# Gated attention and token-MLP on one core: block 0 of X by two transposing DMAs of 256 columns, and the first weights on ACT's queue

## The chip, the cores and the metric

The kernel runs on one core of a Trainium2 chip. The metric is the device time of one execution in microseconds (us); the time before is the median of three timed runs. Next to it there is one profiled execution, whose span (first to last instruction) and whose trace are used for everything that is said of single instructions.

Engines are named as the profile names them: PE is TensorE's matmul and PEld its weight load, DVE is VectorE, ACT ScalarE, POOL GpSimd, SP SyncE. A small q behind a name (SPq, ACTq) marks an instruction of that engine's sequencer, here the issue of a DMA.

## The reference

The input x has 2048 rows (tokens) of 512 columns, in bf16. Two branches are computed from it and mixed by a gate for each row.

```python
def reference(A_x, A_wqkv, A_wo, B_x, B_w1, B_b1, B_w2, B_b2, gate_w):
    x = A_x
    g = _sigmoid((x * gate_w).sum(-1, keepdims=True))
    a = _A_ref(x, A_wqkv, A_wo)
    b = _B_ref(x, B_w1, B_b1, B_w2, B_b2)
    return g * a + (1 - g) * b
```

Branch A is local attention: `qkv = x @ wqkv` (512 x 1536), 32 heads of 16; each token attends to 8 tokens at distances 0, 2, ... 14 behind it; softmax; then `@ wo` (512 x 512). Branch B is a layer norm of x over its columns, then an MLP over the token axis: `u = gelu(h^T w1 + b1)` with w1 of 2048 x 1792, then `u w2 + b2` with w2 of 1792 x 2048, transposed back.

## The kernel before, in words

The kernel lists its operations in Python, each with an engine, an estimated duration, and what it reads and writes (`A = sch.add` for instructions, `sch.dma` for transfers). A list scheduler (`_Sched`) then fixes one static order for each engine from these estimates, from dependences, and from some orders that are written out by hand (`chain(...)`), and puts semaphore waits where data cross engines. For the loads at the start the scheduler's own estimate of a landing is overridden by a number written in the code (`op_.lands = t_`). These numbers shape the planned order; on the chip every instruction waits for the real semaphores.

X lies in SBUF twice: as `X` (tokens on partitions, 16 tiles of 128) for the layer norm, and transposed as `XT` (columns on partitions, 4 pieces of 128 columns, called d=0 to 3, by 2048 tokens) for the projections. XT comes straight from HBM by transposing DMAs, one for each block of 512 tokens: block 0 by `ld_xt0` (L467), blocks 1 to 3 by `ld_xt` (L460). Every other load goes through L429.

TensorE's program in order:

- warm-up matmuls on constants into a PSUM bank that nobody reads yet (L525): nine of 512 columns and one of 256;
- the first projections of block 0 (L593, operations `pf_...`): 8 accumulators, Q and K with 4 output parts each. The Q part goes column piece by column piece: 4 matmuls with d=0, then 4 with d=1, d=2 and d=3; then K with d=0 and 1 (8 matmuls) and with d=2 and 3 (8). So the first 4 matmuls want d=0 of Wq and of block 0, and so on;
- the projections of Q and K of block 1, then of blocks 2 and 3, then V (L593, `pj_...`), with two bursts that sum the attention products (L671);
- the MLP (L785, then L835), and the output projection Wo (L851).

ACT moves the projections out of PSUM (L601 for Q, L604 for K and V) and normalises X (L572). DVE takes the layer norm's statistics (L548, one for each tile of 128 tokens), multiplies Q by shifted K (L663), does the softmax and the weighted sum over V, and combines the branches (L872). DVE's order is written by hand: the statistics of X tiles 0 to 3 come first, then the first product of L663 (`qkm_0_0_0`), which wants Q and K of blocks 0 and 1 evicted by ACT.

The loads at the start, before the change, in the order of issue:

- ACT's queue: Wq, d=0 (`ld_w(0, 0, 1, "act")`);
- SP's queue: block 0 transposed (512 tokens x 512 columns), Wq d=1, d=2, d=3, Wk in two halves, X tiles 0 and 1, block 1 transposed, X tiles 2 and 3, X tiles 4 to 7, block 2, block 3, and the rest.

The two queues feed the same 16 DMA engines of the core. To keep SP's queue from running far ahead, each of SP's later loads waits for the landing of the one five places before it in a list (`throttle`, `init_dmas`).

Of the kernel before, what the change touches and what calls it, by code (L numbers as in the profile page):

```python
# [13 lines left out]
D = 512  # L14
# [4 lines left out]
NST = S // 128  # L19
# [314 lines left out]
def bass_gated_mix__sliding_local_dilated__mixer_token_mlp__prompt_kernel(nc, A_x, A_wqkv, A_wo, B_x, B_w1, B_b1, B_w2, B_b2, gate_w, out, dbg=None):  # L334
    with contextlib.ExitStack() as es:
        view, pview, off, total = _views(nc, es)
        ps = es.enter_context(nc.psum_tensor("ps", [128, 8, 512], FP32))
        esem = {e: es.enter_context(nc.semaphore("sem_" + e)) for e in ("pool", "act", "dve", "pe")}
        sch = _Sched()

        x2d = A_x[0]
# [7 lines left out]
        XT = view("XT", BF16, [(S, 4), (1, S)])  # L349
# [65 lines left out]
        A = sch.add  # L415
# [15 lines left out]
        init_dmas = []  # L431
# [4 lines left out]
        def prev_dma():  # L436
            return [init_dmas[-1]] if init_dmas else []

        def ld_x(t0, n, q="sp"):
            ds = sch.dsem("x%d" % t0)  # L440
            op = sch.dma(q, mk_dma(X[:, t0:t0 + n, :], xv[:, t0:t0 + n, :]), n * 128 * D * 2, ds,
                         writes=["x%d" % t for t in range(t0, t0 + n)], deps=throttle() if q == "sp" else [], after=prev_dma() if q == "sp" else [], name="d_x%d" % t0)
            if q == "sp":
                init_dmas.append(op)
            return op

        def ld_w(tn, d0, n, q="sp"):
            ds = sch.dsem("wqkv%d_%d" % (tn, d0))
            op = sch.dma(q, mk_dma(WQKV[:, d0:d0 + n, tn * D:(tn + 1) * D], wqkv_v[:, d0:d0 + n, tn * D:(tn + 1) * D]),
                         n * 128 * D * 2, ds, writes=["wqkv%d_%d" % (tn, dt) for dt in range(d0, d0 + n)],  # L450
                         deps=throttle() if q == "sp" and n == 4 else [], after=prev_dma() if q == "sp" else [],
                         issue=0.65 if n == 4 else 0.45, name="d_wp%d_%d" % (tn, d0))
            if q == "sp":
                init_dmas.append(op)
            return op
# [5 lines left out]
                         writes=["xt_%d" % t for t in range(4 * sb, 4 * sb + 4)], deps=throttle(), after=prev_dma(), name="d_xt%d" % sb)  # L461
            init_dmas.append(op)

        def ld_xt0(s0, s1):
            ds = sch.dsem("xt0_%d" % s0)
            dst = XT[:, :, s0:s1]
            op = sch.dma("sp", lambda e: e.dma_start_transpose(dst, x2d[s0:s1, :]), (s1 - s0) * D * 2, ds, issue=1.25,  # L467
                         writes=["xt_%d" % t for t in range(s0 // 128, s1 // 128)], after=prev_dma(), name="d_xt0_%d" % s0)
            init_dmas.append(op)
            return op  # L470

        first_loads = [ld_w(0, 0, 1, "act"), ld_xt0(0, 512), ld_w(0, 1, 1), ld_w(0, 2, 1), ld_w(0, 3, 1), ld_w(1, 0, 2), ld_w(1, 2, 2),
                       ld_x(0, 2)]
        ld_xt(1)
        first_loads.append(init_dmas[-1])
        for op_, t_ in zip(first_loads, (2.9, 4.9, 5.4, 5.8, 6.2, 7.0, 7.8, 8.6, 11.0)):
            op_.lands = t_
            op_.deps.clear()
        init_dmas[:] = [first_loads[1]] + first_loads[5:]
        ld_x(2, 2)  # L480
        ld_x(4, 4)
        ld_xt(2)
# [6 lines left out]
        def ld_w1(j):  # L489
# [4 lines left out]
            if j < 4:  # L494
# [8 lines left out]
                       writes=["wo"], deps=throttle(), after=prev_dma(), name="d_wo")  # L503
# [4 lines left out]
        for i_, (v_, n_) in enumerate(((B_b1, NFT), (B_b2, NST))):  # L508
            vr = v_.rearrange("(t q j) -> q t j", q=4, j=32)
            for q_ in range(4):  # L510
                sch.dma("sp", mk_dma(psub(BR, 32 * q_, n_, 32 * i_, [(1, 32)]), vr[q_]), n_ * 64, ds_b, reads=["br"],
                        writes=["br_%d_%d" % (i_, q_)], deps=throttle(), after=prev_dma(), name="d_b_%d_%d" % (i_, q_), issue=0.45)
        d_w1.append(ld_w1(3))
        A("dve", lambda e: e.transpose(out=BT, in_=BR), 0.2, reads=["br_%d_%d" % (i_, q_) for i_ in range(2) for q_ in range(4)],
          writes=["btc"], name="t_b")
# [2 lines left out]

        CONE = nc.const_aps.tensor(1.0, [128, D], BF16)

        def f_warm(n, w_=D):
            def fn(e):
                ins = None
                for _ in range(n):
                    ins = e.matmul(ps[:, 7, 0:w_], lhsT=CONE[:, 0:128], rhs=CONE[:, 0:w_], start=True, stop=True)  # L525
                return ins
            return fn

        A("pe", f_warm(9), 3.84, writes=["lg7_0", "lg7_1"], name="warm1", prio=-100)
        last_tx = A("pe", f_warm(1, 256), 0.2, writes=["lg7_0", "lg7_1"], name="warm2", prio=-100)  # L530

        ALLXT = ["xt_%d" % t for t in range(NST)]

        JK = view("OUTS", BF16, [(1, D)], extra=0)
        def cols(v_, lo, n, step=1):
# [9 lines left out]
        for hf in range(2):  # L545
            t0 = 8 * hf
            for t in range(t0, t0 + 8):
                A("dve", (lambda t_: (lambda e: e.bn_stats(out=ST6[:, t_, :], in_=X[:, t_, :])))(t), 0.59,  # L548
                  reads=["x%d" % t], writes=["st6_%d" % t], name="ln1_%d" % t, prio=0)
# [13 lines left out]
              reads=["zc%d" % hf], writes=["sd%d" % hf], name="ln_sqrt%d" % hf, prio=0)  # L563
            A("dve", (lambda t0_: (lambda e: e.reciprocal(out=cols(RSTD, t0_, 8), in_=cols(SD, t0_, 8))))(t0), 0.25,
              reads=["sd%d" % hf], writes=["rstd%d" % hf], name="ln_rstd%d" % hf, prio=0)
# [43 lines left out]
        for (b0, d0, d1, s0, s1) in ((0, 0, 1, 0, 512), (0, 1, 2, 0, 512), (0, 2, 3, 0, 512), (0, 3, 4, 0, 512), (4, 0, 2, 0, 512), (4, 2, 4, 0, 512)):  # L609
            for b in range(b0, b0 + 4):  # L610
                tn, dl = first[b]
                last_main[0] = A("pe", f_proj(tn, dl, 0, b, d0, d1, s0, s1), 0.216 * (d1 - d0) * (s1 - s0) / 512,
                                 reads=ALLXT[s0 // 128:s1 // 128] + ["wqkv%d_%d" % (tn, dt) for dt in range(d0, d1)],
                                 writes=fbn[b], after=[last_main[0]], name="pf_%s%d_%d_%d" % (tnames[tn], dl, d0, s0))
        for b, (tn, dl) in enumerate(first):
            A("act", f_evq(tn, dl, 0, b), 0.52, reads=fbn[b] + (["k5pad"] if tn == 1 else []),
              writes=["%s5_%d_0" % (tnames[tn], dl)], name="ev_%s%d_0" % (tnames[tn], dl), prio=0)
# [5 lines left out]
        for dl in range(4):  # L623
            seq_proj += [(2, dl, sb) for sb in range(4)]
        for (tn, dl, sb) in seq_proj:
            xr = ALLXT[4 * sb:4 * sb + 4]
            bank = main_bank()
            last_main[0] = A("pe", f_proj(tn, dl, sb, bank), 0.866,
                             reads=xr + ["wqkv%d_%d" % (tn, dt) for dt in range(4)],
                             writes=["acc%d" % bank], after=[last_main[0]], name="pj_%s%d_%d" % (tnames[tn], dl, sb), prio=0)  # L630
            A("act", f_evq(tn, dl, sb, bank), 0.62, reads=["acc%d" % bank] + (["k5pad"] if tn == 1 else ["v5pad"] if tn == 2 else []),
              writes=["%s5_%d_%d" % (tnames[tn], dl, sb)], name="ev_%s%d_%d" % (tnames[tn], dl, sb), prio=0)
# [11 lines left out]
                writes=["xa"] + ["wqkv%d_%d" % (tn, dt) for tn in range(3) for dt in range(4)], name="d_xa")  # L644
        for t in range(NST):
# [5 lines left out]
          writes=["th"], name="g_tanh", prio=0)  # L651
        A("dve", lambda e: e.tensor_scalar(out=G, in0=TH, scalar1=0.5, scalar2=0.5, op0=ALU.mult, op1=ALU.add), 0.15,
          reads=["th"], writes=["g"], name="g_g", prio=0)
        A("dve", lambda e: e.tensor_scalar(out=OMG, in0=TH, scalar1=-0.5, scalar2=0.5, op0=ALU.mult, op1=ALU.add), 0.15,
          reads=["th"], writes=["omg"], name="g_omg", prio=0)
        A("dve", lambda e: e.tensor_tensor(out=C2, in0=OMG, in1=B2C, op=ALU.mult), 0.15,
          reads=["omg", "b2c"], writes=["c2"], name="g_c2", prio=0)
# [25 lines left out]
        for wh in range(2):  # L683
# [6 lines left out]
            for (dl, c0, nc_) in pieces:  # L690
# [3 lines left out]
                  reads=["q5_%d_%d" % (dl, sb) for sb in range(c0, c0 + nc_)] +  # L694
                        ["k5_%d_%d" % (dl, sb) for sb in range(max(c0 - 1, 0), c0 + nc_)] + ["k5pad"],
                  writes=wr, name="qkm_%d_%d_%d" % (wh, dl, c0), prio=0)
            rd = sum([pbn(b_) for b_ in bufs], []) + PBX[wh] + ["rp"]
            for wl in range(4):
                qop = A("pe", f_qkr(list(enumerate(bufs)), (wl,)), 0.92, reads=rd, writes=["lg%d_0" % (4 + wl), "lg%d_1" % (4 + wl)],
                        name="qkr_%d_%d" % (wh, wl), prio=-100 + wl, delay=BURST_DELAY)  # L700
                A("act", (lambda wh_, wl_: (lambda e: e.activation(out=ATT[:, :, 4 * wh_ + wl_, :], in_=ps[:, 4 + wl_, :].rearrange("p (h c) -> p h c", h=2), func=AF.Copy)))(wh, wl),  # L701
                  0.55, reads=["lg%d_0" % (4 + wl), "lg%d_1" % (4 + wl)], writes=["lw%d" % (4 * wh + wl)],
                  name="lev_%d_%d" % (wh, wl), prio=0)
# [24 lines left out]
        for hf in range(2):  # L728
# [3 lines left out]
              reads=["outs1"], writes=["lh%d" % hf] + (wall if hf == 0 else []), name="sm_sub%d" % hf, prio=0)  # L732
            if hf == 0:
                A("act", lambda e: e.activation(out=col(SD, 0), in_=col(ZC, 0), func=AF.Exp, scale=0.0), 1.5,
                  reads=["zc0"], writes=["sd0"], name="sm_pre")
            A("act", (lambda hf_, l_: (lambda e: e.activation(out=ATT[:, hf_], in_=l_, func=AF.Exp)))(hf, lgh), 1.95,  # L736
              reads=["lh%d" % hf], writes=["att%d" % hf], name="sm_exp%d" % hf, prio=0)
# [288 lines left out]
```

## Time and profile before

| | before |
|---|---|
| time, median of 3 runs | 168.22 us (168.10 to 168.66) |
| span of the profiled execution | 167.5 us |
| PE busy | 164.4 us (98%), 858 matmuls |
| DVE busy | 150.9 us (90%) |
| ACT busy | 74.6 us (45%) |
| chain that ended last | PE 94%, DMA 3%, DVE 2% |
| block 0: issue to landing | 4.3 us, SP's issue of it 1.39 us |
| HBM read | 21.11 MB, 139 GB/s over the span |

The profiled execution's own device time is not listed beside its span; the timed runs' median lies 0.7 us above the span, which is what stands around the first and the last instruction. Busy time counts an engine's instructions, not its waiting; a matmul's end is modelled, so that its pace is best read from the starts, or from those of the weight loads. The chain that ended last is followed back from the last instruction to what released each step. All times of instructions count from the span's start.

### The profile page before, as it was taken

The numbers are of one execution on the slowest core, as the hardware profiler recorded it, in microseconds if no ns is written. First come the engines' busy times: TensorE is split into PE (matmuls) and PEld (weight loads), VectorE is DVE, ScalarE is ACT, GpSimd is POOL, SyncE is SP. The second block draws the span as 40 slices with busy tenths as digits, with TensorE's granted clock in tenths as the row PEclk, the third lists the DMA queues.
The fourth block names the chain that finished last, engine by engine and source line by source line (L and its number), as shares of the span: only waits on it lengthen the run. The fifth ranks groups of instructions, "written<-read, shape, count | busy, mean of one in ns | idle before, by whom it ended". The sixth has DMA issues, their size and how long they took to land.

```text
span 167.5 us, 2143 instructions
## 1 busy us (share of the span) xinstructions
PE 164.4 (98%) x858; PEld 77.8 (46%) x858; DVE 150.9 (90%) x153; ACT 74.6 (45%) x115; POOL 0.7 (0%) x8
## 2 busy tenths in 40 slices
PE   8999999999999999999999999999999999999994
PEld 2355555554454444444444444444444444444463
DVE  0035999999899999999999999999999999999896
ACT  3067688889899818793122131131231321310100
POOL 1000000000000000000000000000000000000000
DMA  6999999969003946996789915462672580000454
GB/s 151 280 249 276 310 319 291 302 199 263 0 0 83 323 116 173 304 290 159 172 230 337 342 49 137 117 189 68 182 215 82 142 223 0 0 0 0 157 192 157
DMA packets 47609, 29.64 MB, mean 177 GB/s; under 512 B 9840, under 2 KB 46448, under 8 KB 47600
## 3 DMA queue, kind: packets, MB, share of 16 engines
q1 hardware_dynamic: 45632, 24.98, 54.5%
q10 hardware_dynamic: 1968, 4.52, 9.8%
q8 instruction: 7, 0.11, 0.3%
q14 instruction: 2, 0.02, 0.0%
HBM read 21.11 MB, written 2.10 MB: 139 GB/s over the span
## 4 chain that ended last, share of the span: by engine, by line
PE 94%; DMA 3%; DVE 2%; issue 0%
PE ps L785 29%; PE ps L835 29%; PE ps L593 25%; PE ps L851 6%; PE ps L671 4%; DMA arena<-in_A_x_dram 3%; DVE arena L872 2%
## 5 line engine op out<-in xcount | busy, mean ns | idle before, releaser
L785 PE MATMUL ps<-arena 128*128 128x512 bf16 x224 | 48.7, 380 | 0.0
L835 PE MATMUL ps<-arena 128*128 128x512 bf16 x224 | 48.7, 380 | 0.0
L593 PE MATMUL ps<-arena 128*128 128x512 bf16 x192 | 42.4, 384 | 0.2 <-DMA arena<-in_A_x_dram 0.2
L663 DVE TENSOR_TENSOR arena<-arena 128x4096 bf16<-128x4096 bf16 (+1 forms) x12 | 35.5, 2997 | 2.1 <-ACT arena L604 1.7
L770 DVE TENSOR_TENSOR arena<-arena 128x8192 bf16<-128x8192 bf16 x8 | 35.0, 4420 | 0.0
L835 PEld LDWEIGHTS ps<-arena 128*128 128x128 bf16 x224 | 21.9, 98 | 26.4
L785 PEld LDWEIGHTS ps<-arena 128*128 128x128 bf16 x224 | 21.8, 98 | 26.6 <-ACT arena L701 0.4
L593 PEld LDWEIGHTS ps<-arena 128*128 128x128 bf16 x192 | 21.7, 114 | 21.1 <-issue 1.7
L903 ACT ACTIVATE arena<-ps,arena 128x512 bf16<-128x512 f32 x16 | 12.4, 778 | 39.4 <-PE ps L835 39.4
L773 DVE TENSOR_TENSOR arena<-arena 128x4096 bf16<-128x4096 bf16 (+1 forms) x16 | 27.0, 1753 | 0.0
L604 ACT ACTIVATE arena<-ps 128x512 bf16<-128x512 f32 x32 | 18.5, 596 | 4.5 <-PE ps L593 4.5
L806 ACT ACTIVATE arena<-ps,arena 128x512 bf16<-128x512 f32 x14 | 9.6, 687 | 22.2 <-PE ps L785 16.7
L548 DVE BATCH_NORM_STATS2 arena<-arena 128x6 f32<-128x512 bf16 x16 | 10.0, 681 | 9.6 <-DMA arena<-in_A_x_dram 9.6
L851 PE MATMUL ps<-arena 128*128 128x512 bf16 (+1 forms) x80 | 14.2, 337 | 0.0
L601 ACT ACTIVATE arena<-ps 128x512 bf16<-128x512 f32 x16 | 9.0, 596 | 8.1 <-PE ps L593 8.0
L872 DVE SCALAR_TENSOR_TENSOR arena<-ps,arena 128x512 bf16<-128x512 f32 (+1 forms) x20 | 11.5, 639 | 0.9 <-PE ps L851 0.7
L572 ACT ACTIVATE arena<-arena 128x512 bf16<-128x512 bf16 x16 | 12.2, 804 | 0.0
L851 PEld LDWEIGHTS ps<-arena 128*128 128x128 bf16 x80 | 7.8, 98 | 6.2
L647 DVE SCALAR_TENSOR_TENSOR arena<-arena 128x512 bf16<-128x512 bf16 x16 | 10.1, 687 | 0.0
L717 DVE TENSOR_TENSOR arena<-arena 128x512 bf16<-128x512 bf16 (+4 forms) x11 | 7.3, 667 | 0.6 <-ACT arena L736 0.2
L671 PE MATMUL ps<-arena 128*32 128x512 bf16 x128 | 7.3, 380 | 0.0
L701 ACT ACTIVATE arena<-ps 128x512 bf16<-128x512 f32 x8 | 4.7, 591 | 4.6 <-PE ps L671 4.6
(38 smaller groups left out, 39.8 us busy)
## 6 DMA issues: line engine op xcount, KB each, us to landing
arena<-in_B_w_dram SPq DMA_DIRECT2D x7, 1024.0 KB, 8.3
arena<-in_B_w_dram SPq DMA_DIRECT2D x8, 896.0 KB, 5.2
arena<-arena ACTq DMA_DIRECT2D x32, 128.0 KB, 2.9
arena<-in_A_x_dram SPq DMA_DIRECT2D x4, 512.0 KB, 5.5
out_dram<-arena SPq DMA_DIRECT2D x14, 128.0 KB, 1.7
arena<-in_A_x_dram SPq DMA_DIRECT2D x1, 1536.0 KB, 7.9
arena<-in_A_wqkv_dram SPq DMA_DIRECT2D x2, 256.0 KB, 3.6
arena<-in_A_x_dram SPq DMA_DIRECT2D x2, 256.0 KB, 3.8
```

Source lines behind the costliest of these rows:

```text
L572: A("act", (lambda t_: (lambda e: e.activation(out=X[:, t_, :], in_=X[:, t_, :], func=AF.Identity, scale=col(RSTD, t_), bias=col(NMR, t_)) ...
L593: ins = e.matmul(ps[:, bank, s0:s1], lhsT=lhsT, rhs=XT[:, dt, sb * 512 + s0:sb * 512 + s1], start=(dt == 0 and s0 == 0), stop=(dt == 3))
L604: return lambda e: e.activation(out=dst, in_=ps[:, bank, :], func=AF.Copy)
L663: return lambda e: e.tensor_tensor(out=PBL[buf][:, :, 512 * c0:512 * (c0 + nc_)], in0=in0, in1=in1, op=ALU.mult)
L671: ins = e.matmul(ps[32 * c:32 * c + 32, 4 + wl, :], lhsT=RP, rhs=PBL[buf][:, wl, c * 512:(c + 1) * 512], start=(dl == 0), stop=(dl == 3), ...
L770: A("dve", (lambda o_, i0, i1: (lambda e: e.tensor_tensor(out=o_, in0=i0, in1=i1, op=ALU.mult)))(pv, in0, in1), 4.4, reads=v_res + ["atx_% ...
L773: A("dve", (lambda pv_, n__: (lambda e: e.tensor_tensor(out=pv_[:, 0:n__], in0=pv_[:, 0:n__], in1=pv_[:, n__:2 * n__], op=ALU.add)))(pv, n ...
L785: ins = e.matmul(ps[:, bank, :], lhsT=W1W[:, slot, st, 128 * e_:128 * e_ + 128], rhs=X[:, st, :], start=(st == 0), stop=(st == NST - 1))
L835: ins = e.matmul(ps[:, bank, :], lhsT=W2S[slot][:, ft, 128 * e_:128 * e_ + 128], rhs=UT[:, ft, :], start=(ft == 0), stop=(ft == NFT - 1))
L851: ins = e.matmul(ps[:, bank, 0:c1 - c0], lhsT=OT[:, t, 128 * i:128 * i + 128], rhs=WO[:, t, c0:c1], start=(t == 0), stop=(t == 3))
L872: A("dve", (lambda i_, b_, c0_, c1_: (lambda e: e.scalar_tensor_tensor(out=T1[:, i_, c0_:c1_], in0=ps[:, b_, 0:c1_ - c0_], scalar=col(G, i ...
L903: A("act", (lambda i_, bank_: (lambda e: e.activation(out=T1[:, i_, :], in_=ps[:, bank_, :], func=AF.Identity, scale=col(OMG, i_), bias=co ...
```

## The change

It alters the loads at the start and the warm-up, and nothing else in what is computed.

- `ld_xt0(h)` now loads 256 columns: all 512 tokens of block 0, column pieces 2h and 2h+1. Two of them stand back to back on SP. Their landings are told apart by d (`XT0`, `xt_of`), so that the matmuls with d=0 and 1 wait for the first and those with d=2 and 3 for the second.
- Wq's quarters d=1, 2, 3 go from SP's queue to ACT's, behind a wait for the landing of quarter d=0.
- Block 1's transposing DMA goes ahead of X tiles 0 and 1 on SP.
- The warm-up has 7 matmuls of 512 columns in place of 9 and one of 256.
- The planned landings and one planned issue time are other numbers. By this and by the rest the scheduler's order on ACT changes in a few places (the normalisations L572 of tiles stand one or two evictions later); the orders of PE and DVE are the same but for the warm-up.

In the changed kernel all lines from the projections on are numbered 8 higher (L593 becomes L601, L671 becomes L679), and the warm-up's line is L530.

```diff
-        def ld_xt0(s0, s1):
-            ds = sch.dsem("xt0_%d" % s0)
-            dst = XT[:, :, s0:s1]
-            op = sch.dma("sp", lambda e: e.dma_start_transpose(dst, x2d[s0:s1, :]), (s1 - s0) * D * 2, ds, issue=1.25,
-                         writes=["xt_%d" % t for t in range(s0 // 128, s1 // 128)], after=prev_dma(), name="d_xt0_%d" % s0)
+        def ld_xt0(h):
+            ds = sch.dsem("xt0_%d" % h)
+            dst = XT[:, 2 * h:2 * h + 2, 0:512]
+            op = sch.dma("sp", lambda e: e.dma_start_transpose(dst, x2d[0:512, 256 * h:256 * h + 256]), 512 * 256 * 2, ds, issue=1.2,
+                         writes=["xt0_%d" % d for d in (2 * h, 2 * h + 1)], after=prev_dma(), name="d_xt0_%d" % h)
             init_dmas.append(op)
             return op
 
-        first_loads = [ld_w(0, 0, 1, "act"), ld_xt0(0, 512), ld_w(0, 1, 1), ld_w(0, 2, 1), ld_w(0, 3, 1), ld_w(1, 0, 2), ld_w(1, 2, 2),
-                       ld_x(0, 2)]
+        first_loads = [ld_w(0, 0, 1, "act"), ld_xt0(0), ld_xt0(1)]
+        first_loads += [ld_w(0, d_, 1, "act") for d_ in range(1, 4)]
+        first_loads += [ld_w(1, 0, 2), ld_w(1, 2, 2)]
         ld_xt(1)
         first_loads.append(init_dmas[-1])
-        for op_, t_ in zip(first_loads, (2.9, 4.9, 5.4, 5.8, 6.2, 7.0, 7.8, 8.6, 11.0)):
+        first_loads.append(ld_x(0, 2))
+        for op_, t_ in zip(first_loads, (2.9, 3.9, 5.2, 4.8, 5.3, 5.7, 6.7, 7.5, 10.4, 11.2)):
             op_.lands = t_
             op_.deps.clear()
-        init_dmas[:] = [first_loads[1]] + first_loads[5:]
+        for a_, b_ in zip(first_loads[3:5], first_loads[4:6]):
+            b_.order.add(a_)
+        first_loads[3].deps.add(first_loads[0])
+        init_dmas[:] = [first_loads[2]] + first_loads[6:]
...
-        A("pe", f_warm(9), 3.84, writes=["lg7_0", "lg7_1"], name="warm1", prio=-100)
-        last_tx = A("pe", f_warm(1, 256), 0.2, writes=["lg7_0", "lg7_1"], name="warm2", prio=-100)
-
-        ALLXT = ["xt_%d" % t for t in range(NST)]
+        A("pe", f_warm(7), 2.99, writes=["lg7_0", "lg7_1"], name="warm1", prio=-100)
+
+        XT0 = ["xt0_%d" % d for d in range(4)]
+        ALLXT = XT0 + ["xt_%d" % t for t in range(4, NST)]
+
+        def xt_of(sb, d0=0, d1=4):
+            return XT0[d0:d1] if sb == 0 else ["xt_%d" % t for t in range(4 * sb, 4 * sb + 4)]
...
-                                 reads=ALLXT[s0 // 128:s1 // 128] + ["wqkv%d_%d" % (tn, dt) for dt in range(d0, d1)],
+                                 reads=xt_of(0, d0, d1) + ["wqkv%d_%d" % (tn, dt) for dt in range(d0, d1)],
...
-            xr = ALLXT[4 * sb:4 * sb + 4]
+            xr = xt_of(sb)
```

## The prediction

> **What bounds the kernel now.** I read the chain of waits first: it tells which engine sets the end, and where anything else does.
>
> ```profile
> 15 pieces in order of time: start us, us, what
> 0.73 0.07 issue
> 0.80 4.34 DMA arena<-in_A_x_dram
> 5.14 0.14 issue
> 5.27 33.60 PE ps L593 x152
> 38.88 3.57 PE ps L671 x64
> ...
> 161.94 0.03 issue
> 161.97 3.98 DVE arena L872 x9
> ```
>
> From 5.27 us to 161.94 us the chain is TensorE without a break (94% of the span). Ahead of it stand 4.34 us of one DMA: block 0 of X, transposed (L467). The first real matmul waits for it, and every later piece follows from that matmul. So I read the timeline of the first microseconds next; its columns are start, length, engine, line, operation, tiles, count, idle time before.
>
> ```profile
> 0.80 0.38 ACTq L429 DMA_DIRECT2D arena<-in_A_wqkv_dram  x1
> 0.80 1.39 SPq L467 DMA_TRANSPOSE arena<-in_A_x_dram  x1
> 0.84 4.21 PE L525 MATMUL ps<-const-bfloat16-1.0 128*128 128x512 bf16 x10 [0.84 <-PEq L1011]
> ...
> 3.78 0.15 PEld L525 LDWEIGHTS ps<-const-bfloat16-1.0 128*128 128x128 bf16 x1 [0.28 <-issue]
> 4.20 0.15 PEld L525 LDWEIGHTS ps<-const-bfloat16-1.0 128*128 128x128 bf16 x1 [0.27 <-issue]
> ...
> 5.24 0.14 PEld L593 LDWEIGHTS ps<-arena 128*128 128x128 bf16 x2 [0.89 <-issue]
> ...
> 5.66 0.15 PEld L593 LDWEIGHTS ps<-arena 128*128 128x128 bf16 x1 [0.27 <-issue]
> 6.08 0.15 PEld L593 LDWEIGHTS ps<-arena 128*128 128x128 bf16 x1 [0.27 <-issue]
> 6.51 9.44 PEld L593 LDWEIGHTS ps<-arena 128*128 128x128 bf16 x44 [0.27 <-issue]
> ```
>
> Two things are to be seen. The warm-up matmuls (constants, L525) fill the wait from 0.84 to 5.05 us. And the pace changes late: weight loads stand 0.427 us apart through the warm-up and still at 5.24, 5.66, 6.08 and 6.51; behind that 44 of them take 9.44 us, 0.216 us each. The switch from half to full pace, placed by the one interval of 0.26 us between the two, falls at about 6.6 us, 5.8 us after TensorE began. So some 1.3 us of real work run at half pace, three matmuls in the time of six. (The granted clock in the windows view says 1.00 throughout; only the pace shows it.)
>
> Third, bytes in half-microsecond windows (the last column is GB/s, the one before it the DMA share):
>
> ```profile
> 2.00:2.50 0.50, 0.50 (x3) 0.15 (x2) 0.00 (x0) 0.49 (x1) 0.00 (x0) 1.00 0.94 260
> 2.50:3.00 0.50, 0.50 (x3) 0.23 (x2) 0.00 (x0) 0.00 (x0) 0.00 (x0) 1.00 1.27 255
> 3.00:3.50 0.50, 0.50 (x3) 0.22 (x2) 0.00 (x0) 0.00 (x0) 0.00 (x0) 1.00 1.28 289
> 3.50:4.00 0.50, 0.50 (x3) 0.15 (x2) 0.00 (x0) 0.00 (x0) 0.00 (x0) 1.00 1.28 290
> ```
>
> The first Wq quarter (131 KB) is through by 2.5 us. Of the transposed 524 KB about 30 KB are there at 2.5, 156 at 3.0, 301 at 3.5, 446 at 4.0; so half of it at 3.4 and all at 4.25, and the landing told at 5.14 is 0.9 us behind the last byte.
>
> **The change, part by part.**
>
> *Block 0 in two halves of 256 columns.* What TensorE waits for first is now d=0 of Wq and the first half. The half's landing is not in the trace; I bound it. Late end: nothing but its own bytes is saved, so 3.4 + 0.9 = 4.3 us. Early end: the bytes begin only when SP's issue ends (1.39 us for the whole, ends 2.19, bytes from about 2.3), and half the descriptors take half the issue; then all comes 0.7 us sooner, 3.6 us. Beyond both lies 5.1 us, if a transposing DMA costs the same whatever its width. I take 4.0, between the first two, as I can't tell how much of the issue goes with width. The first matmul follows a landing by 0.14 us (5.14 to 5.27): it starts at 4.15 instead of 5.27.
>
> *The warm-up falls from 9.5 matmuls to 7.* They end at 0.84 + 7 x 0.427 less 0.05 = 3.78 us, so TensorE stands idle for 0.37 us before 4.15, where it stood 0.22 us before. The shorter warm-up costs nothing by itself as long as the half lands after 3.64.
>
> *What the earlier start is worth.* If full pace still comes at 6.6 us, the 1.12 us gained are run at half pace: 1.12 / 0.427 = 2.6 matmuls, which no longer have to be run later at 0.216 us: 0.57 us. So a microsecond of earlier start is worth 0.506 us, not one; this is the main term. On the early end the start is 3.78 and the gain 0.76; on the late end (4.43) it is 0.43; with no gain in the landing it is 0.
>
> *Wq's last three quarters on ACT's queue, behind a wait for the first.* They leave SP's queue, where they took three issues of 0.42 to 0.75 us; on ACT they start when the first has landed (3.02 us). Behind this wait on ACT stand only the activation table's load (1.28 us) and the first eviction, which ran at 8.91; three issues of some 0.45 us from 3.07 end at 4.4, the table at 5.7: hidden. Their landings: the first quarter took 2.2 us alone, the others 2.7 to 3.3 us in a loaded queue. From issues at 3.07, 3.5 and 4.0 this gives 5.3 to 6.4, 5.7 to 6.8, 6.2 to 7.3. TensorE needs d=1 at 4.15 + 4 x 0.427 = 5.86, d=2 (and the second half of block 0) at about 7.1, d=3 at 7.95. Only d=1 can be late, by up to 0.6 us, at half pace worth up to 0.3 us. Wq's second quarter now shares the engines with block 0's second half alone, not with a queue of three; I take 5.6 and nothing for it.
>
> *The second half* is issued behind the first on SP. Even if its bytes wait until the whole block was through before and Wq's come in between, 5.14 + 0.5 is far ahead of 7.1. Nothing.
>
> *X's first tiles behind block 1.* Block 1 (landed at 11.45, wanted at 12.8, from now on at 12.2) moves ahead of 256 KB and comes earlier. The first X tiles landed at 9.50 and VectorE read them at 9.53; they now come after block 1, about 11 to 11.5 us. The pair behind them has the same bytes ahead as before (landed 12.35). Four BATCH_NORM_STATS2 of 0.69 us end by 13.7 or 14.2. VectorE's next step waits for ACT:
>
> ```profile
> 15.37 4.50 DVE L663 TENSOR_TENSOR arena<-arena 128x4096 bf16<-128x4096 bf16 x2 [1.71 <-ACT arena L604]
> ```
>
> that is, for TensorE, and moves to 14.8. Cover of 0.6 us at the least; it is gone if the first tiles land after 12.06 us. Nothing.
>
> *Whether the gain reaches the end.* VectorE is 90% busy and could hold the rest back. Its two anchors are TensorE's: the row above, and the one at 42.50, where it had been idle for 0.42 us waiting for L671. That burst began at 38.81, while the last product it needs had ended at 37.65: 1.16 us of slack on that side. Both move with TensorE. The order of PE and DVE is otherwise unchanged; on ACT a few normalisations stand one or two evictions later, in a stretch where TensorE did not wait for them.
>
> Sum: 0.57 us off a span of 167.5 gives 166.9. The three timed runs have a median of 168.22, 0.7 us more than the span, which lies around it; so 168.22 - 0.57 = 167.65. What a measurement of this kernel can tell from no change is 0.3%, 0.5 us: the forecast stands just beyond it, and the half must land by 4.14 us for that.
>
> **The rivals.**
>
> *Full pace comes later (slower).* TensorE's idle time before the first real matmul grows from 0.22 to 0.37 us, and to 0.65 on the late end. If that is too much for whatever releases the pace, and the 5.8 us count anew from 4.15, full pace comes at about 9.9 instead of 6.6: 3.3 us more at half pace, 3.3 x (1 - 0.506) = 1.63 us, less the 0.57: 169.3. It decides from a switch at 7.75 us on. Against it: 0.22 us did not seem to matter. Chance 0.08. The Trainium skill, "TensorE: Matmul & The Clock Gate", Part 1, says that the clock opens after a busy window of 3413 ns, free-running, so that the moment varies; by that page one missed window costs 3.41 x 0.494 = 1.69 us, an estimate of 169.3 as well. The trace's 5.8 us agrees with a first window that TensorE only partly filled, which is one execution and no proof.
>
> *Full pace comes earlier in other executions (faster).* If it is there before 4.15, the whole 1.12 us is gained: 167.1. The timed runs spread over 0.56 us, which such a varying moment could make. Chance 0.08.
>
> *The half lands hardly earlier (same).* If it lands between 4.14 and 5.14, the gain is 0 to 0.5 us: about 167.95. For it: the landing is 0.9 us behind the bytes and the bytes 1.5 us behind the issue, both perhaps fixed; only 0.9 us of 4.34 surely go with size. Chance 0.30. The Trainium skill, "DMA: Bandwidth & Descriptors", Rules for kernel authors, speaks against the split: many small transfers are to be coalesced into one. By that rule block 0 as a whole comes later; the time would then be 168.2 or more if the first matmul needed the whole, but it needs a half.
>
> *ACT's wait makes Wq late (slower).* Each quarter must be 1.1 us later than needed to eat the gain (d=1 after 7.0 us, against 6.4 at most): with it, X's tiles too late for VectorE. About 168.8; together 0.08.
>
> **How the numbers follow.** Main case 0.46 (167.45 to 167.71), earlier pace 0.08: faster 0.54. Hardly earlier landing: same 0.30. Late pace and late loads: slower 0.16. I leave out the late pace (169.3) and part of the late loads above, and the last of the earlier pace below: 167.05 to 168.6.
>
> **What would show it.** Right: the first L467 lands at about 4.0, the first L601 matmul stands at about 4.15 with five or six at 0.427 us, the switch still at about 6.6, no wait for a Wq quarter, VectorE's first long product at about 14.8, TensorE unbroken to its end. Wrong: a landing near 5, a gap before the fifth matmul, a switch beyond 7.7, or a wait for VectorE at the first burst of L679.

## The result, and the profile after

The changed kernel takes 170.24 us (median of 4 runs, 169.94 to 170.75), the kernel before 168.43 us in the runs beside it (168.10 to 168.66): a ratio of 1.0113, interval 1.0089 to 1.0138. The forecast was 167.65 us, faster; it is 1.8 us slower (1.9 by the ratio). Ratios and ranges below leave out one execution each of e1 (171.38 us) and e2 (171.34 us) that were sorted out as slow by their time alone.

The chain of waits of the changed kernel, answering to the one shown of before (start, length, what):

```profile
0.80 3.73 DMA arena<-in_A_x_dram
4.53 0.14 issue
4.67 35.77 PE ps L601 x152
...
163.53 3.98 DVE arena L880 x9
```

The first real matmul does start earlier, at 4.67 instead of 5.27 us. But the same 152 matmuls now take 35.77 us where they took 33.60, and the last piece starts 1.56 us later. Nothing after them differs. So the loss lies in the first stretch of projections, and the timeline of the first 16 us shows where:

```profile
0.80 2.65 SPq L467 DMA_TRANSPOSE arena<-in_A_x_dram  x2
0.84 3.14 PE L530 MATMUL ps<-const-bfloat16-1.0 128*128 128x512 bf16 x7 [0.84 <-PEq L1019]
...
4.64 0.14 PEld L601 LDWEIGHTS ps<-arena 128*128 128x128 bf16 x2 [1.56 <-issue]
...
6.48 0.15 PEld L601 LDWEIGHTS ps<-arena 128*128 128x128 bf16 x2 [0.85 <-DMA arena<-in_A_wqkv_dram]
...
9.46 0.15 PEld L601 LDWEIGHTS ps<-arena 128*128 128x128 bf16 x1 [0.28 <-issue]
...
9.89 0.15 PEld L601 LDWEIGHTS ps<-arena 128*128 128x128 bf16 x1 [0.28 <-issue]
10.28 5.72 PEld L601 LDWEIGHTS ps<-arena 128*128 128x128 bf16 x27 [0.25 <-issue]
```

Weight loads stand 0.427 us apart up to 9.89 us; only behind 10.2 us do they come every 0.216 us. In the kernel before that switch fell at 6.6. By the starts of the matmuls TensorE pauses from 3.78 us (end of the seventh warm-up matmul) to 4.67: 0.89 us, against 0.43 us before (4.84 to 5.27). The load at 6.48 waits for Wq's second quarter; 0.15 us of that is lost.

The sum of these rows is the whole difference of the two profiled executions: the earlier start at half pace, 0.605 x 0.506 = 0.31 us gained; the wait for Wq at half pace, 0.08 us; the switch later by 10.24 - 6.60 = 3.64 us, each costing 0.494: 1.80 us. Together +1.57 us, and the last piece of the chain is 1.56 us later.

The line of the transposing DMAs and the bytes in half microseconds show what became of the first half:

```profile
L467 SPq DMA_TRANSPOSE arena<-in_A_x_dram x2: 1280/1298/1317, 0.8 to 2.2; - x2
...
DMA to landing us min/median/max: 3.7/4.1/4.5
```

```profile
3.00:3.50 0.50, 0.50 (x3) 0.07 (x1) 0.00 (x0) 0.00 (x0) 0.00 (x0) 1.00 1.03 218
3.50:4.00 0.50, 0.48 (x2) 0.00 (x0) 0.00 (x0) 0.00 (x0) 0.00 (x0) 1.00 0.60 144
4.00:4.50 0.50, 0.00 (x0) 0.00 (x0) 0.00 (x0) 0.15 (x1) 0.00 (x0) 1.00 1.20 189
```

The issue of half a block takes 1.28 to 1.32 us, that of the whole 1.39. Two halves hold SP for 2.65 us, and the DMA engines move less: 275 KB from 3.0 to 4.5 us, where the kernel before moved 448 KB. The half landed at 4.53, the second at 6.67.

VectorE's first long product, behind the evictions, slipped with TensorE; it still waits for ACT, not for X:

```profile
16.93 2.29 DVE L671 TENSOR_TENSOR arena<-arena 128x4096 bf16<-128x4096 bf16 x1 [1.85 <-ACT arena L612]
```

One more number of the kernel before belongs here. In later runs of it the span is listed beside the time: 166.9 us with 168.12, 167.1 with 168.40, 167.8 with 169.04, so about 1.25 us lie around the span, not 0.7. The profiled execution of before, span 167.5, was thus one of its slower ones. With full pace from the first real matmul on (5.27 us) its span would be (6.60 - 5.27) x 0.494 = 0.66 us shorter, 166.9 us, an estimate that fits the usual execution; no trace here shows one.

### The profile page after: what moved, and what is told of

It is laid out like the page before. It is cut to its first block, busy times and chain, and to the rows that moved or that the text cites. A ratio compares the mean times of both kernels' runs of the same rounds, so it can differ in the third digit from the quotient of the medians.

```text
span 169.1 us, 2139 instructions
## 1 busy us (share of the span) xinstructions
PE 165.5 (98%) x855; PEld 77.5 (46%) x855; DVE 150.7 (89%) x153; ACT 74.7 (44%) x115; POOL 0.7 (0%) x8
## 4 chain that ended last, share of the span: by engine, by line
PE 94%; DVE 2%; DMA 2%; issue 0%
PE ps L793 29%; PE ps L843 29%; PE ps L601 26%; PE ps L859 6%; PE ps L679 4%; DVE arena L880 2%; DMA arena<-in_A_x_dram 2%
## 5 line engine op out<-in xcount | busy, mean ns | idle before, releaser
L793 PE MATMUL ps<-arena 128*128 128x512 bf16 x224 | 48.7, 379 | 0.0
L843 PE MATMUL ps<-arena 128*128 128x512 bf16 x224 | 48.7, 379 | 0.0
L601 PE MATMUL ps<-arena 128*128 128x512 bf16 x192 | 44.6, 396 | 0.7 <-DMA arena<-in_A_x_dram 0.7
L671 DVE TENSOR_TENSOR arena<-arena 128x4096 bf16<-128x4096 bf16 (+1 forms) x12 | 35.5, 2996 | 2.3 <-ACT arena L612 1.9
L601 PEld LDWEIGHTS ps<-arena 128*128 128x128 bf16 x192 | 21.8, 115 | 23.8 <-issue 4.6
L880 DVE SCALAR_TENSOR_TENSOR arena<-ps,arena 128x512 bf16<-128x512 f32 (+1 forms) x20 | 11.5, 637 | 0.9 <-PE ps L859 0.7
L679 PE MATMUL ps<-arena 128*32 128x512 bf16 x128 | 7.3, 380 | 0.0
```

Of the source, the lines that this page charges most:

```text
L601: ins = e.matmul(ps[:, bank, s0:s1], lhsT=lhsT, rhs=XT[:, dt, sb * 512 + s0:sb * 512 + s1], start=(dt == 0 and s0 == 0), stop=(dt == 3))
L671: return lambda e: e.tensor_tensor(out=PBL[buf][:, :, 512 * c0:512 * (c0 + nc_)], in0=in0, in1=in1, op=ALU.mult)
L679: ins = e.matmul(ps[32 * c:32 * c + 32, 4 + wl, :], lhsT=RP, rhs=PBL[buf][:, wl, c * 512:(c + 1) * 512], start=(dl == 0), stop=(dl == 3), ...
L793: ins = e.matmul(ps[:, bank, :], lhsT=W1W[:, slot, st, 128 * e_:128 * e_ + 128], rhs=X[:, st, :], start=(st == 0), stop=(st == NST - 1))
L843: ins = e.matmul(ps[:, bank, :], lhsT=W2S[slot][:, ft, 128 * e_:128 * e_ + 128], rhs=UT[:, ft, :], start=(ft == 0), stop=(ft == NFT - 1))
L880: A("dve", (lambda i_, b_, c0_, c1_: (lambda e: e.scalar_tensor_tensor(out=T1[:, i_, c0_:c1_], in0=ps[:, b_, 0:c1_ - c0_], scalar=col(G, i ...
```

## The experiments

Theory A: the pause of TensorE ahead of its first real matmul puts off the full pace. Rival B: the loads cost the time (the split, the wait on ACT's queue, X's tiles). The "pause" is taken from the starts of matmuls throughout.

**e1: the pause filled.** The changed kernel with nine warm-up matmuls.

```diff
-        A("pe", f_warm(7), 2.99, ...)
+        A("pe", f_warm(9), 3.84, ...)
```

> The changed kernel with nine warm-up matmuls in place of seven. They end at about 4.63 us, just where the first half of block 0 landed (4.53, first matmul at 4.67), so the idle time of 0.89 us ahead of the first real matmul is gone. Theory A (the idle time put off the full pace, from 6.6 to 10.2 us): the switch is back at about 6.6 us, 3.6 us x 0.494 = 1.8 us come back, and the start that is 0.6 us earlier gives 0.3 us beside the kernel before: 0.2 to 0.3 us below it, about 168.2 us. Rival B (the split block, the wait on ACT's queue or the later X tiles cost the time): it stays at about 170.2 us, and the switch stays where it is.

Measured 169.32 us, ratio to before 1.0048 (1.0023 to 1.0073). Weight loads of TensorE in the profiled execution:

```profile
6.34 0.15 PEld L601 LDWEIGHTS ps<-arena 128*128 128x128 bf16 x1 [0.28 <-issue]
6.77 0.34 PEld L601 LDWEIGHTS ps<-arena 128*128 128x128 bf16 x2 [0.28 <-issue]
```

There is no pause (first real matmul at 4.63), and the switch falls at 6.8 us. So it was the idle time ahead of the first real matmul that made the switch late, and filling it gives 0.9 of the 1.9 us back (before had 168.36 us in these runs). But 1.0 us stays, which theory A had not expected: at full pace TensorE now waits for loads, 0.30 us for the third Wq quarter (landed 7.59), 0.06 for the fourth, and 0.32 us at 20.5 us for block 3 of X (landed 20.95; 18.15 before). The last of these waits is not the change's alone: it comes up in e9 too, with the loads of before.

**e2: the pause alone.** The kernel before with seven warm-up matmuls, all loads as before.

> The kernel before with seven warm-up matmuls alone, all its loads as they were. TensorE is then idle from 3.78 to 5.27 us, 1.5 us. Theory A: the switch comes at 10 us or later, and the time is at least 1.7 us above the kernel before (3.5 us x 0.494), about 170.2 us. Rival B: the loads are as before, so the time is that of the kernel before, 168.4 us.

Measured 170.14 us, ratio 1.0088 (1.0062 to 1.0113); the pause is 1.44 us, the switch at 8.9 us:

```profile
8.59 0.15 PEld L592 LDWEIGHTS ps<-arena 128*128 128x128 bf16 x1 [0.28 <-issue]
8.95 0.98 PEld L592 LDWEIGHTS ps<-arena 128*128 128x128 bf16 x5 [0.21 <-issue]
```

A shorter warm-up alone does nearly as much harm as the whole change, so rival B is out as the only cause. The pause here is longer than the changed kernel's 0.89 us; for a pause of that size e1 is the test.

**e3: a hole early in the warm-up**, to tell how the full pace is released.

```diff
-        A("pe", f_warm(9), 3.84, ...)
-        last_tx = A("pe", f_warm(1, 256), 0.2, ...)
+        A("pe", f_warm(3), 1.28, ..., name="warm1", prio=-100)
+        A("pe", f_warm(4), 1.71, reads=["wqkv0_0"], ..., name="warm2", prio=-100)
```

> The kernel before with a hole of about 1 us early in the warm-up: three matmuls (0.84 to 2.07 us), a wait for the first Wq quarter (3.0 us), then four more to about 4.9 us, and the first real matmul at 5.27 as before. It tells apart how the full pace is released. A1 (TensorE has to run some 5.8 us without a longer break, counted anew behind one): the switch falls at about 3.15 + 5.75 = 8.9 us, and the time is 2.3 x 0.494 = 1.1 us longer, 169.5 us. A2 (a window of fixed length has to be mostly busy, and the one that counted ran from about 3.2 to 6.6 us): the early hole lies ahead of it, the switch stays at 6.6 us and the time at 168.4 us. The Trainium skill, TensorE: Matmul & The Clock Gate, Part 1, gives the window as 3413 ns and free-running; by it the switch may also fall elsewhere in single executions.

Weight loads of TensorE in the profiled execution:

```profile
1.22 0.15 PEld L525 LDWEIGHTS ps<-const-bfloat16-1.0 128*128 128x128 bf16 x1 [0.28 <-issue]
3.02 0.13 PEld L525 LDWEIGHTS ps<-const-bfloat16-1.0 128*128 128x128 bf16 x2 [1.65 <-DMA arena<-in_A_wqkv_dram]
...
6.38 2.54 PEld L593 LDWEIGHTS ps<-arena 128*128 128x128 bf16 x12 [0.28 <-issue]
```

The hole is 0.96 us long (2.07 to 3.03), and the switch still falls at 6.5 us, 3.5 us behind the hole (a pause of 0.40 us, as before, lies between): no unbroken 5.8 us are needed, A1 is out as the rule. But A2's time, 168.4 us, is missed: the median is 169.58 us (ratio 1.0067, 1.0041 to 1.0093; 168.74 to 170.76), near what A1 gave, and the profiled execution is the fastest of the ten. In three of the ten about 1.1 us more than usual lie outside the span; the spans alone have a median of 168.0 us, against 167.1 of before, so that in other executions the switch seems to fall later. That would agree with a window that is not tied to the kernel's start and fails where it takes in the hole; no trace of a slower execution shows it.

**e9 and e10: doses of the pause.** The kernel before without its last small warm-up matmul; the changed kernel with eight.

> A dose of idle time between the two that are known: the kernel before without the last warm-up matmul of 256 columns. By the starts of the matmuls its pause ahead of the first real one was 0.43 us (4.84 to 5.27); here it is 0.64 us. In the kernel before the times run from 168.03 to 169.1 us, as a switch that falls anywhere between about 3.8 and 7.2 us would give. Theory A2 (some window of 3.4 us must be mostly busy, the share at which it counts lying between 74% and 87%): at a pause of 0.64 us a window that holds all of it is 81% busy. If that is enough, the time stays at 168.4 us, with the same spread; if not, the switch moves behind the pause, to 8 to 11.5 us, and the time is 169.3 to 171.1 us, about 170.1 in the middle. Theory A1 (only an unbroken run counts): with 0.43 us already survived it would not say where between.

> The dose from the other side: the changed kernel with eight warm-up matmuls, a pause of 0.45 us ahead of the first real one, like that of the kernel before. Theory A2: a pause of this size is survived, so the switch comes between 4 and 7.2 us again, and the time is that of the version with nine, 169.3 us; what is left of the loss is then the loads' alone. If any pause beyond the 0.43 us counts against it, the time is that of the changed kernel, 170.2 us.

e9: 168.29 us, ratio 1.0006 (0.9993 to 1.0019): no loss. e10: 169.39 us, ratio 1.0065 (1.0039 to 1.0091): that of the version with nine. In both profiled executions the pause was 0.58 us, and the switch had come by 5.5 us. So 0.58 us, behind eight or nine warm-up matmuls, does no harm, and 0.89 us behind seven does; whether the longer pause or the shorter warm-up decides, these runs don't separate. The trace of e9 shows one thing more. Its switch is 1.1 us earlier than in the profiled execution of before, yet its span is the same 167.5 us: block 3 of X landed at 20.37 us (18.15 there), and TensorE lost 0.50 us waiting for it. The chain of waits of e9:

```profile
15.37 5.00 DMA arena<-in_A_x_dram
...
20.51 18.29 PE ps L592 x84
```

**e5, e6, e7: one part of the change at a time**, on the kernel before with its full warm-up.

```diff
 e5: Wq on ACT's queue
+        first_loads += [ld_w(0, d_, 1, "act") for d_ in range(1, 4)]
...
+        first_loads[2].deps.add(first_loads[0])
 e6: ld_xt(1) ahead of ld_x(0, 2)
 e7: ld_xt0(0), ld_xt0(1) ahead of Wq on SP; f_warm(9)
```

> The kernel before (whole block 0, full warm-up, X ahead of block 1) with one part of the change alone: Wq's last three quarters on ACT's queue behind the landing of the first. They landed at 5.9 to 6.4, 7.1 to 7.6 and 8.6 to 8.8 us in the changed kernel and in its version with nine warm-up matmuls; TensorE, started at 5.27 us, wants them at about 6.1 to 7.0, 7.0 to 7.9 and 7.9 to 8.7. Theory C (the chained quarters cost some of what the longer warm-up did not give back): a wait of 0.2 to 0.7 us at the second to fourth group, 168.5 to 169.1 us. Rival (they are hidden): 168.4 us.

Measured 169.63 us, ratio 1.0064 (1.0044 to 1.0084), above the expected range. TensorE's waits:

```profile
PEld ps L597 <- DMA arena<-in_A_wqkv_dram: 2.1, 3, 1.2
```

Three groups of the Q projection wait for their quarter, landed at 6.97, 7.95 and 8.99 us (5.52, 5.87, 6.21 before); the pace is full here from the first real matmul on, so that 1.2 us are lost, as much as the medians say. The second quarter took 3.9 us from issue to landing: while ACT waited for the first (until 3.01 us), SP had already issued Wk, and from 4.0 to 5.0 us SP's queue moved 0.25 MB and ACT's nothing.

> The kernel before with one part alone: X tiles 0 and 1 behind block 1 on SP's queue. Theory D (this order makes the issue of blocks 2 and 3 later; with nine warm-up matmuls block 3 landed at 20.95 us and TensorE waited 0.32 us for it): block 3 lands 1.5 to 2 us later than the 18.15 us of before, at 19.7 to 20.2, about when TensorE wants it (20.6), a wait of 0 to 0.3 us: 168.4 to 168.7 us. Rival (X's first tiles reach VectorE too late): VectorE's first long product starts later than TensorE's eviction allows, by 0.5 us or more, with a wait of TensorE at the first burst.

Measured 168.51 us, ratio 0.9996 (0.9981 to 1.0012): no difference. X's first tiles landed at 11.83 us, block 3 at 19.78, 1.6 us later than before and still in time. This part is hidden, as both the prediction and theory D had it.

> One part alone with the wait filled: block 0 in two halves back to back on SP, nine warm-up matmuls, Wq's other quarters on SP behind the halves, X ahead of block 1. The first matmul starts at about 4.65 us without idle time. Wq's second quarter is issued at 3.5 us instead of 2.25 and lands at about 6.3 to 6.8, while TensorE wants it at 5.5 (full pace) to 6.3 (half pace). Theory E (the second transposing issue of 1.3 us on SP is paid by what stands behind it): a wait of 0.3 to 1 us at the fifth matmul takes the 0.3 to 0.6 us of the earlier start back: 168.1 to 168.7 us. Rival (the earlier half is worth its time): 167.8 to 168.0 us.

Measured 169.38 us, ratio 1.0048 (1.0032 to 1.0064), slower than even theory E had it. TensorE starts at 4.67 us and then waits for what stands behind the two halves on SP:

```profile
PEld ps L596 <- DMA arena<-in_A_wqkv_dram: 1.5, 2, 1.0
...
PEld ps L596 <- DMA arena<-in_A_x_dram: 0.8, 1, 0.8
```

By the starts of the matmuls 0.28, 0.17 and 0.50 us are lost at these waits. Wq's second quarter landed at 6.57 (5.52 before), the first half of Wk at 9.43 (7.02), block 1 of X at 13.41 (11.45). Behind the second transposing issue they are issued 1.1 to 1.3 us later than before, and they land 1.0 to 2.4 us later.

**e8: a version meant to beat both.** Wq's second quarter between the two halves, the other two on ACT's queue, nine warm-up matmuls.

> A version meant to beat both: as the one before it, but Wq's second quarter stands between the two halves on SP (issue at 2.2 us, landing at about 5), and the third and fourth go to ACT's queue behind the first (landing at about 6 and 7). Nothing should be late: TensorE starts at 4.65 us, idle nowhere, and wants the quarters and the second half at 5.5 to 6.3, 6.4 to 7.5 and 7.2 to 8.2. The gain over the kernel before is the 0.62 us of the earlier start, at half pace 0.3: 167.8 to 168.1 us. If the second half, now issued at 2.9 us, lands after 7 us, TensorE waits for it and the time is that of the kernel before.

Measured 169.65 us, ratio 1.0069 (1.0041 to 1.0096). Wq's second quarter landed at 6.08 us, not at 5, which cost 0.28 us; the second half landed at 7.97 us, and TensorE waited 1.0 us for it. A miss: even the case that was allowed for, a late second half at the time of the kernel before, came out 1.2 us too low.

**e11 and e12: what the issue of a transposing DMA goes with.** Halves by tokens; quarters by columns (one run).

> Block 0 in two halves by tokens in place of columns: two transposing DMAs of 256 tokens and all 512 columns, back to back on SP; the first four matmuls become eight of 256 columns, four for each half; nine warm-up matmuls, everything else as in the kernel before. It tells what the issue of a transposing DMA goes with. 512 tokens cost 1.39 us at 512 columns and 1.32 or 1.28 at 256. If the issue goes with the tokens (0.7 us each), the second ends at 2.25 us as the whole did, nothing behind is later, the first half lands at 3.9 to 4.3 us, the first matmul starts at 4.63, and the time is 0.2 to 0.6 us below the kernel before: 167.8 to 168.2 us. If each costs 1.3 us whatever its size, the loads behind are 1.3 us late as in the version split by columns: 169.3 us.

> One look at block 0 in four transposing DMAs of 128 columns, else as the version split in two with nine warm-up matmuls. Theory E (the issue does not go with the columns): four issues of 1.2 to 1.3 us, Wq's second quarter issued at about 6 us instead of 3.5, and a time about 1.5 to 2.5 us above the version in halves (169.4 us), near 171 to 172 us. If the issue goes with the columns below 256 (0.65 us each), it is that of the halves, 169.4 us.

e11: 169.14 us, ratio 1.0046 (1.0031 to 1.0062); the two issues took 1.31 and 1.29 us. e12: 173.62 us in one run, span 172.3, beyond the 171 to 172 of theory E; its row of issues, and the weight loads behind Wq's late second quarter:

```profile
L467 SPq DMA_TRANSPOSE arena<-in_A_x_dram x4: 1225/1246/1262, 0.8 to 4.7; - x4
```

```profile
4.20 0.81 PEld L596 LDWEIGHTS ps<-arena 128*128 128x128 bf16 x4 [0.28 <-issue]
8.61 0.14 PEld L596 LDWEIGHTS ps<-arena 128*128 128x128 bf16 x2 [3.60 <-issue]
...
14.55 1.41 PEld L596 LDWEIGHTS ps<-arena 128*128 128x128 bf16 x7 [0.26 <-issue]
```

128, 256 or 512 columns, 256 or 512 tokens: 1.2 to 1.4 us each. For these first transposing DMAs of the queue the issue is a fixed price, to within 0.17 us over four times the bytes. The rest of e12's loss is TensorE's pace: it had been full, and after the wait from 5.3 to 8.6 us it was half until 14.5.

**e4, e13, e14: the wait on ACT's queue taken away.**

```diff
-        first_loads[3].deps.add(first_loads[0])
 e13, e14 in its place:
+        first_loads[3].order.add(first_loads[0])
```

> The changed kernel without the wait on ACT's queue: Wq's last three quarters are issued right behind the first. In the changed kernel the quarter d=1 landed at 6.44 us and the fifth real matmul stood 0.15 us late for it. Theory A: the quarters land earlier and that gap goes, worth about 0.08 us, while the first half of block 0, whose bytes now share the engines with them, lands up to 0.5 us later, worth 0.25 us the other way; the late pace stays: 170.0 to 170.5 us. Rival B (the chained Wq loads are what costs): 1.5 us or more come back, 168.6 us.

e4: 170.53 us, ratio 1.0105 (1.0074 to 1.0136), but it settles nothing on the wait: without any tie among them, the quarter d=0 was issued third, and the first matmul stood until 6.13 us for it.

> The changed kernel without the wait on ACT's queue, with Wq's quarters issued in the order d=0, 1, 2, 3 at 0.8, 1.2, 1.7 and 2.2 us. (In the earlier try without the wait the quarter d=0 had slipped to the third place, so that the first matmul waited for it until 6.13 us.) Wq's 393 KB now share the engines with block 0's first half. Theory A (the pause costs): the first half lands at 5.0 us as in that try, the pause grows from 0.89 to about 1.4 us, the full pace stays late, between 8 and 11.5 us: 169.6 to 171 us. If the wait on ACT was what cost, 168.6 us.

> The same with nine warm-up matmuls, so that the pause is about 0.5 us, which was survived. Against the version with nine and the wait (169.3 us) it tells what the wait is worth. If the wait on ACT holds the 1.0 us that the longer warm-up did not give back: Wq's quarters land by about 4.5, 5.5 and 6.5 us, TensorE waits for none of them, and the time is 168.2 to 168.5 us. If the second transposing issue on SP and the bytes do (the second half landed at 8.4 us in the earlier try, and TensorE wants it at about 6.7 to 7.4): a wait of about 1 us for the second half takes the place of the one for Wq, and the time stays at 169 to 169.5 us.

e13: 169.65 us, ratio 1.0081 (1.0055 to 1.0106); the first half landed at 5.29 us, the pause is 1.65 us, the switch at 9.0 us. e14: 169.53 us, ratio 1.0078 (1.0061 to 1.0096), not better than with the wait (169.32). Wq's quarters came earlier (5.39, 6.07, 7.09 us), the two halves later (5.57, 7.63). TensorE's weight loads:

```profile
5.67 1.44 PEld L601 LDWEIGHTS ps<-arena 128*128 128x128 bf16 x8 [1.75 <-issue]
7.68 6.41 PEld L601 LDWEIGHTS ps<-arena 128*128 128x128 bf16 x31 [0.56 <-DMA arena<-in_A_x_dram]
```

The first half lands later here than the whole block did before (5.14), and the second is waited for. So the wait on ACT's queue does not hold the rest of the loss by itself: with it Wq is late, without it block 0 is. What the first groups need are the same bytes either way, and fewer of them flow: from 2.0 to 5.0 us the DMA engines moved 638 KB in e14, 681 KB in the changed kernel and 820 KB in the kernel before. With the wait, the low stretch is the one between the two halves (144 GB/s from 3.5 to 4.0 us); without it the DMA share is 1.20 in that stretch (0.60 with it), so the engines were not short of work there, and why they moved less is not shown. These rows also show a pause of 1.07 us (4.63 to 5.71) behind which the pace is full at once; whether it was released ahead of the pause or in it can't be read from them.

## Why the prediction was wrong

*The half's landing* is the step that failed first. I took 4.0 us, between an early end where the issue halves with the width and a late end where it doesn't. It doesn't (e7, e11, e12), and 4.53 us is 0.2 beyond even the late end of 4.3. The early end had no row behind it: the trace of before held transposing DMAs of one size only, and I read a price per issue as a price per descriptor.

*The pause* was forecast as 0.37 us and measured at 0.89. The whole error comes from the landing. Beside it the comparison was of unlike measures: the 0.22 us of before go by the modelled end of the last warm-up matmul, while the like of the 0.37 is 0.43 us, by starts. So the forecast pause was no longer than that of before, and the rival rested on the late end. Whether 0.37 us behind only seven warm-up matmuls would have been harmless, no run shows.

*"If full pace still comes at 6.6 us"* was the condition of the main term and did not hold. The rival named for it, full pace later, is what happened, with a chance of 0.08; its switch of 9.9 us was near (10.24), its reason in the main, though a count of 5.8 us that starts anew is not the rule (e3). Its time (169.3) was 0.9 us low. Half of that is the later landing (0.26 us), the later switch (0.17) and the wait for Wq (0.08); most of the rest is that the rows of the sum come from the profiled execution of before, which the listed spans show to be one of the slower, while the sum starts from the median time. That execution was also my only evidence that a pause does no harm. The price of a microsecond at half pace (0.506 gained, 0.494 lost) held: by it the rows sum to 1.57 of 1.56 us. The other rival on the pace, full pace earlier, was priced by the start alone (1.12 us); on a trace with the switch at 6.6 us the half pace behind 5.27 us would have gone too, another 0.66 us by the same price.

The Trainium skill, "TensorE: Matmul & The Clock Gate", Part 1, has a free-running window of 3413 ns; the runs agree with it better than with my 5.8 us after the start. Full pace came 3.5 to 3.7 us behind the long pause in e13, e2 and e3, 5.6 in the changed kernel, 5.8 in e4, all within some one to two such windows, and with the first real matmul in e5 and e14, behind nine warm-up matmuls or more. That the moment varies for the same work of TensorE, the traces do show: five profiled executions have the same nine warm-up matmuls, one every 0.427 us up to 3.35 us, and the switch at 3.7 (e11), 4.3 (e12), 5.3 (e8) and 6.8 us (e1, e7). In e11 it lies inside the warm-up, which ends half a microsecond earlier than in e7; the row of e11, then that of e7:

```profile
0.84 3.50 PE L525 MATMUL ps<-const-bfloat16-1.0 128*128 128x512 bf16 x9 [0.84 <-PEq L1010]
```

```profile
0.84 4.00 PE L525 MATMUL ps<-const-bfloat16-1.0 128*128 128x512 bf16 x9 [0.84 <-PEq L1014]
```

These are five kernels that differ in their loads alone up to there, one execution of each. That a free-running window is the reason is not shown; a run of e2 at 168.3 us where all others are above 169.8 would fit it too.

*Wq on ACT's queue* was taken at 5.6 us for the second quarter, from a range of 5.3 to 6.4; it landed at 6.44. It did share the engines with block 0's second half alone, as I had it, but it did not get its share: issued at 3.01 us, ACT's queue moved nothing until 4.5 us, while SP's moved the transposed bytes. By 5.5 us 0.11 MB had come on ACT's queue, and SP's moved almost nothing from 5.0 to 6.0, so Wk was not ahead of it. With the same issues the quarter landed at 5.86 us in e1, so its landing varies by half a microsecond. In e5, where SP issues Wk at 2.25 us, SP's bytes go first too. At half pace the late quarter cost 0.08 us; at full pace the chained quarters alone cost 1.2 us (e5). The half pace hid this load path: with the pause filled, the loss turned into waits for loads (e1, e10).

*The second half* was bounded by 5.14 + 0.5 = 5.64 us, far ahead of 7.1; it landed at 6.67, a microsecond beyond the bound. Still ahead of 7.1, so nothing was lost, but the margin was 0.4 us and not 1.5, and in e8 and e14 it was waited for. *X behind block 1*: the first tiles came at 12.59 us, not 11 to 11.5, and past the limit of 12.06 that I gave; no harm, since TensorE and with it VectorE's own due time were late as well. By itself the part costs nothing (e6). *The gain reaches the end*: right in its mechanism; the 1.56 us of loss reached the end undiminished.

The Trainium skill's rule that the prediction set against the split ("DMA: Bandwidth & Descriptors", Rules for kernel authors) is to coalesce many small transfers into one large, and it puts the mark at 64 KB. A half has 262 KB, so that the split did not pay here is no test of that rule; the runs show the price of the issue (1.3 us).

What stays open: the times of e1 (168.3 to 170.8 us) and e10 (168.6 to 170.6) spread more than those of before, and one trace each doesn't show which waits make the slower ones. Why the switch falls where it falls stays open as well. No version here beats the kernel before.

## What to carry to other kernels

A shorter wait for the first data is worth only half while TensorE runs at half pace, and any idle time that it opens between warm-up and first matmul can cost several times as much: size the warm-up to last until the measured landing. With eight warm-up matmuls or more, full pace had come by 6.8 us in all eleven profiled executions here; with seven and a pause of 0.89 to 2.4 us, it came at 8.9 us or later in all four. Before a transfer is split, look at what its issue costs on the queue: if the price is per issue, each split is paid by everything behind it. And one profiled execution is one draw; put its span beside those of the timed runs before a sum is made on it.

## What the runs showed of the hardware

- The issue of a transposing DMA at the head of SP's queue took 1.23 to 1.39 us for 131 to 524 KB, against 0.41 to 0.58 us for most plain ones (up to 0.75 right behind a transposing one); blocks 1 to 3, issued later with other loads ahead, took 1.7 to 5.1 us each. With two halves back to back the DMA engines moved 144 GB/s in the half microsecond between them, where they had moved 290.
- A pause of 3.3 us threw TensorE back to half pace: in e12 (one execution) it ran at full pace by 4.5 us, waited for Wq from 5.3 to 8.6, and needed until 14.5 us for full pace again.
- The moment of full pace varies for the same work: 3.7 to 6.8 us in five executions with the same nine warm-up matmuls.
- The kernel before, whose loads and instructions are the same in each run, spreads over 1 us (168.03 to 169.10); by the price of half pace (0.494) a switch that varies by 2.2 us would make all of it, an estimate. Waits for block 3 of X can make part of it: 0.50 us in the profiled execution of e9, with the loads of before.
